# V once per 128 tokens, its rows moved to the key groups by transfers within SBUF

## The chip, the cores and the metric

The kernel runs on one core of a Trainium2 chip. The metric is the device time of one execution in microseconds (us): the median of repeated runs, and beside it one execution that the hardware profiler recorded, whose span and traces are quoted below.

## The reference

One transformer block with adaptive layer norm. The input `x` is 2048 tokens of 448 features; a conditioning vector `c` gives six modulation vectors through `silu(c) @ w_mod`. The first half is a sliding, dilated attention with 16 heads of 28 features, in which each token looks at itself and at seven earlier tokens, two apart; the second half is an MLP of width 1792.

```python
h = _layernorm(x) * (1 + ca) + sa
qkv = h @ wqkv                                  # 2048 x 3 x 16 x 28
idx = pos[:, None] - off[None, :]               # off = 0, 2, ..., 14
logits = einsum('bhsd,bhswd->bhsw', q, k[idx]) * 28 ** -0.5
o = einsum('bhsw,bhswd->bhsd', softmax(where(idx >= 0, logits, -1e9)), v[idx])
x = x + ga * (o @ wo)
h = _layernorm(x) * (1 + cb) + sb
y = _layernorm(h)
x = x + gb * (gelu(y @ w1 + b1) @ w2 + b2)
```

## The kernel before, in words

**Streams and tiles.** Since the offsets are all even, the even and the odd tokens are two independent streams (`NS` = 2) of 1024 tokens, in which a token looks at itself and the seven before it (`WIN` = 8). A tile `p` is 128 tokens of each stream; there are eight. For each tile the kernel loads `x`, normalizes it, transposes it (on PE for tiles 0 to 3, by `DMA_TRANSPOSE` on SP's queue for 4 to 7), applies the modulation into `hT` (features on the partitions), and computes Q and K. For tiles 2 to 7 (`natural_qk`, lines 615 to 636) Q and K come out with tokens on the partitions and are transposed by two `DMA_TRANSPOSE` on SP's queue into `qT` and `kT`.

**Batches.** Attention (`attention`, line 686) goes in nine batches of 114 queries per stream: two groups `j` of 57 queries (`WQ`), and each group has its 64 keys (`WK`), since the first query needs seven earlier tokens. The keys of group 0 sit on partitions 0 to 63, those of group 1 on 64 to 127. A batch computes the logits (`lt`, L742), their exponentials on ACT (L749), the mask on DVE (L755), the sums (`pd`, L764) and the product with V (`po`, L775); ACT turns the sums into reciprocals (L784, L786) and DVE multiplies (`omul`, L792) into `qT`, from where the output projection reads. 

**V before.** For the product, V must lie in the same two groups: `vb` is 128 partitions of 64 + 64 keys, by streams, heads and 32 features. The seven keys at the seam lie in both groups. For batches 1 to 8 the copy `windows` (L694) first puts the two windows of `hT` side by side into `hw`; V of the batch is then one product per stream against `Wv` (L552 for three full row blocks, L558 for the rest of 64 rows), and ACT or DVE evacuates it into `vb` (L725, L728). Batch 0 (`DIRECT`) takes the windows straight out of `hT` with products of 64 columns each (L710).

**Behind attention.** The modulation rows `ga`, `sb`, `g2`, `gb` are made on PE (L645), evacuated by ACT into `mod_rows` (L650), stored by SP into a DRAM buffer `mod_hbm` (L652) and read back by SP, broadcast over the partitions, as `mod_bc` (L654). DVE multiplies `wo_s`, the output weights, by `ga` (`wo_scale`, L657). The output projection of tile `p` (`pw`, L807) needs `wo_s` so scaled and the batches that cover the tile; then come the residual and two layer norms on DVE (L814 and on), a transpose on SP's queue (`yT`, L838), and in three phases the MLP (`p`, L552, L558 and L887; gelu on ACT, L868).

**What sets the order.** Every piece is a numbered task with its engine or a choice of engines. Two tables written out in the file decide everything: `ORDER` is the sequence in which the tasks are issued (and with a letter the engine of a task that has a choice), `SLOTS` the buffer that each takes. Each engine and each DMA queue works through its own tasks in that order. Entries such as `243+5@243` put small products of zeros (L390) in front of a task. SP issues the loads, the transposes and the stores in one queue; ACT's queue has only the loads of `c` in it.

Of the kernel before, what the change touches and what calls it, by code (L numbers as in the profile page):

```python
# [37 lines left out]
ROOM = {"P": 4, "et": 2, "den": 2, "zy": 5, "h2": 3, "yT": 3, "hm": 2, "vb": 3, "xp": 3, "hw": 2}  # L38
SPLIT = 2
DIRECT = range(0, 1)  # L40
# [12 lines left out]
64 66 79 67 88:A 111 21 65 68+2@68 109 69 70 22 23 85:P 26 112 110 80 89:P 113 81 82 90 27 95+16@95 114 86 91 116 92 102  # L53
103 115 83 104 87:A 96 84 97 117:A 118 93:A 98 120:A 119 94:P 41 36 28 121:A 122 100 30 105 107 106 135 137 138 136 99
139 123+1@123 133 108 147 242:P 145 140 148 101 146 149 142 134 29 141 150 31 151 152 204 124 126 125 127 191 192 202 32
189:R 194 33 143:A 203 205 34 190 153 154 144 206 207 156 155:A 158 128 157:A 129 35 195 214 131 212 40 130 8 163 208
209 210:D 132 211 291 292 37 164 165 193 196 215 160 246 247 213 249 159 250 216 248 197 251 175 281 161 198 166 217 219
218 220 252 38 176 199 289 200 254 168 282 290 293 162 167 279 280 294 243+5@243 244 169 201 283 177 319:P 284 172 323
324 295 221 326 171 245:D 320 286 39 178 285 255 327 321 170 222 225 253 223 325 224 226 173 287 296 393 328 329 322 297
256 288 330 331 356 332 227 231 179 230 232 174 228 298 180 257 333 49 302:A 258 261 51 259 334 335 360 363 394 364 238  # L60
357 395 262 260 263 338 300:A 361 264 358 336 266 265 299:A 301:A 396 339 337 239 240 267 308 340 307 365 268 271 269
341 343 270 342 359 303 229 309 233 272 344 273 46 586:P 304 44 43 588 397 345 362 400 305 401 587 235 367 274 276 398
275 589 241 346 366 368 234 47 236 348 347 349 277:D 350 471:P 369 472 45 399 402 403 315 351 353 352 316 354:D 370 405
54 188 473 278 355 53 404 406 407 371 185 474 408 372 373 375 317 431 183 432 374 376 450 508:A 430 377 436 435 378 187
449 42 409 410 451 412 434 181 437 411 433 452 438 441 444 380 442 443 413 414 379 381 382 385 386 383 50 440 439 306
384 453 415 184 416 52 318 446 186 445 447 310 48 182 417 387 388 418 419 237 422 456 466 420 475 478 464 448 470 479
476 457 423 421 424 467 425 427 515 516 512 390 389 391:D 426 513 465 392 428:D 509 477 480 429 481 312 468 517 510 311
514 518 511:D 519 483 482 313:D 484 520 521 545 547 546 550 485 522 523 524 486 549 551 558 559 527 548 487 563 561 568
571 488 454 489 528 469 560 490 491 562 314 553 552 557 554 555 623:P 570 565 625 492 624 626 564 556 460 493 525 590
494 495 496 497 500 526 529 501 530 531 498 499 566 567 585 455 572 569 630 532 533 534 502 593 594 595 535 537 591 458  # L70
631 538 592 536 459 461 462 503 627 596 598 539 540 628 579 632 505 580 599 629 633 635 597 541 634 542 543:D 504 506:D
581 600 636 637 601 582 638 602 603 583 639 544 640 507 661 641 662 642 643 644 604 605 606 607 608 610 660 665 645 646
647 648 649 652 664 609 611 612 666 663 653 615 613 614 668 667 669 672 670 463 671 673 674 677 678 676 680 679 682 616
573 617 618 681 683 619 620 690 688 696 650 651 654 686 655 656 657 574 658:D 621:A 694 622 684 675 689 685 691 692 687
575 576 659 718 577 701 719 720 721 700 697 704 695 702 703 706 698 705 699 707 708 584 578 709 713 722 726 725 724 711
710 693 712 717 715 729 716 714 737 727 730 738 739 728 733 734 723 731 740 732 735 741 742 736 743 744
# [87 lines left out]
def kernel(  # L164
# [32 lines left out]
    def fixed(room, tiles):  # L197
        return P.buf(room, lambda k: tiles[k])
# [32 lines left out]
    one1 = cst.tile([1, 128], BF16, name="one1")  # L231
# [4 lines left out]
    warm_w = cst.tile([128, 512], BF16, name="warm_w")  # L236
# [6 lines left out]
    vbufs = [cst.tile([128, NS, H, HP], BF16, name=f"vb{i}") for i in range(ROOM["vb"])]  # L243
    wm_st = sb("hm", [128, 2 * KT - 2, D], BF16, "wm_st")
# [55 lines left out]
    def consts():  # L300
        for vb in vbufs:
            nc.vector.memset(vb[:, :, :, DH:HP], 0.0)
        nc.vector.memset(ones_k[:], 1.0)
        nc.vector.memset(ones_k[0:WIN - 1, 1, :], 0.0)
# [90 lines left out]
    def c_cols():  # L395
        for k in range(KT):
            nc.tensor.matmul(psc.t[:, 0, 128 * k:128 * k + 128], lhsT=c_row[0:1, k * 128:(k + 1) * 128], rhs=one1[:], start=True, stop=True)
# [284 lines left out]

    def attention(i, tbl, prev_w1):
        q00 = i * SBQ
        ps_ = covers(q00 - (WIN - 1), q00 + SBQ + WK - WQ)
        kc = LEAD + q00 - (WIN - 1)
        vb = fixed("vb", vbufs)
        pv = psum("pv")
        if i not in DIRECT:
            hw = sb("hw", [128, KT, NS, 2, WK], BF16, "hw")  # L690

            def windows(copy):
                for j in range(2):
                    copy(out=hw.t[:].rearrange("p k s j c -> p (k s) j c")[:, :, j], in_=hT[:, :, kc + j * WQ:kc + j * WQ + WK])  # L694

            add("DVE", 0.46, lambda: windows(nc.vector.tensor_copy), port=True, reads=["pads"] + [f"h{kt}_{p}" for kt in range(KT) for p in ps_],
                bufs=[hw], fills=[hw], name="windows",
                alt={"ACT": (1.12, lambda: windows(nc.scalar.copy)), "POOL": (1.18, lambda: windows(nc.gpsimd.tensor_copy))})
            summed([(lambda s=s: pv.t[:, s, 0:D], lambda kt, rows, s=s: hw.t[rows, kt, s].rearrange("p j c -> p (j c)"),
                     lambda kt, rows: Wv[rows, kt, :]) for s in range(NS)], 0.1895, ["wv", "wvr0", "wvr1"],  # L700
                   [pv, vb, hw], [pv], f"v{i}")
        else:
            def vmm(kts, first):

                for s in range(NS):
                    for kt in kts:
                        rest = kt == KT - 1
                        rows = slice(KS * s, KS * s + KS) if rest else slice(0, 128)
                        for j in range(2):
                            nc.tensor.matmul(pv.t[WK * j:WK * j + WK, s, 0:D], lhsT=hT[rows, NS * kt + s, kc + j * WQ:kc + j * WQ + WK],  # L710
                                             rhs=Wv[rows, kt, :], start=first and kt == kts[0], stop=not first and kt == kts[-1],
                                             tile_position=(rows.start, WK * j))

            def v_last():
                vmm(range(KT - 1), True)
                vmm([KT - 1], False)

            def v_first():
                vmm([KT - 1], True)
                vmm(range(KT - 1), False)  # L720

            add("PE", 7 * 0.1895 + 0.1, None, reads=["pads", "wv", "wvr0", "wvr1"] + [f"h{kt}_{p}" for kt in range(KT) for p in ps_], bufs=[pv, vb],
                fills=[pv], instr=32, name=f"v{i}",
                alt={"PE": (7 * 0.1895 + 0.1, v_last, "128x64", "64x64"), "PE2": (7 * 0.1895 + 0.1, v_first, "64x64", "128x64")})
        add("ACT", 0.80, lambda: nc.scalar.copy(out=vb.t[:, :, :, 0:DH],  # L725
                                                in_=pv.t[:, :, 0:D].rearrange("p s (h d) -> p s h d", h=H)),
            reads=["vpad"], bufs=[pv, vb], fills=[vb], name="evac_v",
            alt={"DVE": (1.0, lambda: nc.vector.tensor_copy(out=vb.t[:, :, :, 0:DH],  # L728
# [237 lines left out]
```

## Time and profile before

| | us |
|---|---|
| median of 3 runs | 168.84 (168.84 to 168.95) |
| the profiled execution | 169.01 |
| its span in the trace | 167.3 |
| PE busy | 161.9 of the span |
| DVE, ACT, POOL busy | 121.0, 104.4, 48.4 |

The span runs from the first to the last instruction in the trace; 1.7 us of the profiled execution lie around it. Busy times of PE are of pipelined products, so a full PE is not yet a PE at its peak. The chain of work that ended last, and the timelines of PE, DVE, ACT and SP's queue, say more than the busy shares: they tell which wait stood at the end of each stage.

### The profile page before, as it was taken

Reading aid. Unit: us, or ns where it says so; the run is one execution under the profiler, and the core shown is the slowest. Engines: PE = TensorE matmul, PEld = TensorE weight load, DVE = VectorE, ACT = ScalarE, POOL = GpSimd, SP = SyncE. Lnnn points to the kernel's source line nnn. Section 1 sums busy time; section 2 is a strip of 40 time slices with the busy share of each in tenths; the row PEclk is TensorE's granted clock in tenths of the full one; section 3 lists DMA queues with packets and bytes.
Section 4 is the critical chain, followed back from the end, with each engine's and each line's share of the span. In section 5 each row is a group of like instructions: output and inputs, shape, how many; then the busy total and the mean of one; then the engine's idle time right before and its main releaser. Section 6 shows DMA issues by size and latency. Waiting matters only on the chain.

```text
span 167.3 us, 4993 instructions
## 1 busy us (share of the span) xinstructions
PE 161.9 (97%) x2121; PEld 84.5 (51%) x2121; DVE 121.0 (72%) x297; ACT 104.4 (62%) x145; POOL 48.4 (29%) x77
## 2 busy tenths in 40 slices
PE   6999999999999999999999999999999999999992
PEld 4767745455545443355544345464335554444651
DVE  6969999898999799978849679869797714020041
ACT  3267999777899976897872698670566100637300
POOL 5025514420157004180006574200304800090000
PEclk9999999999999999999999999999999999999999
DMA  5999839898997789206750000084000330023011
GB/s 156 299 276 319 323 73 135 187 214 203 158 276 205 157 184 239 52 0 35 151 67 2 4 0 4 0 76 109 4 0 0 65 63 0 4 106 113 0 69 41
DMA packets 33462, 18.26 MB, mean 109 GB/s; under 512 B 26395, under 2 KB 32480, under 8 KB 33440
## 3 DMA queue, kind: packets, MB, share of 16 engines
q1 hardware_dynamic: 33436, 17.95, 48.9%
q8 instruction: 16, 0.26, 0.7%
q14 instruction: 6, 0.05, 0.1%
q10 hardware_dynamic: 4, 0.00, 0.0%
HBM read 9.81 MB, written 1.84 MB: 70 GB/s over the span
## 4 chain that ended last, share of the span: by engine, by line
PE 87%; DMA 5%; SPq 2%; DVE 2%; ACT 2%; issue 0%; ACTq 0%
PE p L887 26%; PE p L552 22%; PE pq L552 10%; PE pw L807 7%; PE pv L552 5%; PE p L558 4%; PE lt L742 3%; DMA wqk_st<-in_A_wqkv_dram 3%; PE po L775 3%; PE pq L558 2%; DMA kT<-zy 2%; PE pd L764 1%; ACT et L749 1%; PE pv L710 1%; PE pv L558 1%; PE ptr L539 1%
## 5 line engine op out<-in xcount | busy, mean ns | idle before, releaser
L868 ACT ACTIVATE hm<-p,b_col 128x512 bf16<-128x512 f32 x56 | 34.0, 690 | 34.0 <-PE p L558 29.6
L887 PE MATMUL p<-w_s,hm 128*128 128x448 bf16 (+1 forms) x238 | 44.3, 342 | 0.0
L552 PE MATMUL p<-yT,w_s 128*128 128x512 bf16 x168 | 38.6, 380 | 0.0
L478 POOL TENSOR_TENSOR rs_all<-tv_all,neg_half 128x2 f32<-128x2 f32 x22 | 18.2, 830 | 56.7 <-DVE tv_all L476 56.5
L887 PEld LDWEIGHTS <-hm 128*128 128x128 bf16 x238 | 22.8, 98 | 19.1 <-issue 0.2
L893 DVE TENSOR_TENSOR x_all<-p,x1p 128x896 bf16<-128x896 f32 (+2 forms) x10 | 9.0, 904 | 25.2 <-PE p L887 25.2
L552 PEld LDWEIGHTS <-w_s 128*128 128x128 bf16 x168 | 15.8, 98 | 21.0 <-issue 3.4
L462 DVE BATCH_NORM_STATS2 stt<-x_all 128x6 f32<-128x448 bf16 x32 | 18.9, 616 | 0.3
L749 ACT ACTIVATE et<-lt 128x928 bf16<-128x928 f32 x18 | 16.3, 942 | 2.6 <-PE lt L742 2.5
L845 POOL TENSOR_TENSOR x1p<-x_all,gbb_bc 128x448 f32<-128x448 bf16 x16 | 16.4, 1049 | 0.0
L552 PE MATMUL pq<-wqk_st,hT 128*128 128x448 bf16 x72 | 15.5, 354 | 0.0
L807 PE MATMUL pw<-wo_s,qT 128*128 128x448 bf16 x64 | 12.9, 353 | 0.0
L814 DVE TENSOR_TENSOR x_all<-pw,x_all 128x896 bf16<-128x896 f32 x8 | 8.7, 1084 | 4.1 <-PE pw L807 4.1
L755 DVE TENSOR_TENSOR et<-et,mask 128x928 bf16<-128x928 bf16 x18 | 11.1, 634 | 0.7 <-ACT et L749 0.6
L792 DVE TENSOR_TENSOR qT<-po,den 128x912 bf16<-128x912 f32 x9 | 9.8, 1103 | 1.7 <-ACT den L786 1.2
L784 ACT ACTIVATE den<-pd 128x928 f32<-128x928 f32 x9 | 8.5, 944 | 4.1 <-PE pd L764 4.1
L823 DVE TENSOR_TENSOR h<-h,mod_bc 128x896 bf16<-128x896 bf16 x16 | 10.7, 668 | 0.4
L552 PE MATMUL pv<-Wv,hw 128*128 128x448 bf16 x48 | 10.4, 353 | 0.0
L632 ACT CAST zy<-pq 128x896 bf16<-128x896 f32 x11 | 9.9, 911 | 0.5 <-PE pq L552 0.2
L482 DVE TENSOR_SCALAR zy<-h,mvs,rs_all 128x448 bf16<-128x448 bf16 x16 | 7.9, 532 | 2.5 <-POOL rs_all L478 2.4
L786 ACT ACTIVATE den<-den,den_bias 128x928 f32<-128x928 f32 x9 | 9.6, 1068 | 0.2
L462 DVE BATCH_NORM_STATS2 stt<-h 128x6 f32<-128x448 bf16 x16 | 9.5, 617 | 0.2
(117 smaller groups left out, 190.2 us busy)
## 6 DMA issues: line engine op xcount, KB each, us to landing
w_s<-in_B_w_dram SPq DMA_DIRECT2D x7, 224.0 KB, 3.2
out_dram<-x_all SPq DMA_DIRECT2D x7, 224.0 KB, 2.1
x_all<-in_A_x_dram SPq DMA_DIRECT2D x3, 448.0 KB, 6.8
wmod<-in_w_mod_dram SPq DMA_DIRECT2D x3, 448.0 KB, 6.6
w_s<-in_B_w_dram SPq DMA_DIRECT2D x3, 448.0 KB, 4.6
wqk_st<-in_A_wqkv_dram SPq DMA_DIRECT2D x3, 225.0 KB
wm_st<-in_w_mod_dram SPq DMA_DIRECT2D x1, 672.0 KB
x_all<-in_A_x_dram SPq DMA_DIRECT2D x2, 224.0 KB, 3.8
```

Source lines behind the costliest of these rows:

```text
L462: add("DVE", 0.53, lambda: nc.vector.bn_stats(out=stt[:, w, b, :], in_=src()), reads=reads, bufs=bufs, after=early if w == b == 0 else (), ...
L478: add("POOL", 0.55 + 0.17 * n, lambda: nc.gpsimd.tensor_tensor(out=r, in0=tv, in1=neg_half[:, 0:n], op=ALU.pow), reads=[f"tv{w}_{b0}", "ne ...
L552: nc.tensor.matmul(out(), lhsT=lhs(kt, slice(0, 128)), rhs=rhs(kt, slice(0, 128)), start=first and kt == 0, stop=not first and kt == KT - 2)
L558: nc.tensor.matmul(out(), lhsT=lhs(KT - 1, rows), rhs=rhs(KT - 1, rows), start=first, stop=not first, tile_position=(rows.start, 0))
L632: add("ACT", 0.80, lambda to=to, src=src: nc.scalar.copy(out=to(), in_=src()), bufs=[pq, st], reads=["zpad"], writes=[(st, 0)], name="evac ...
L749: exps.append(add("ACT", 0.83, lambda half=half, lt=lt: nc.scalar.activation(out=et.t[:, 2 * half:2 * half + 2].rearrange("p r m c -> p r ...
L755: nc.vector.tensor_tensor(out=ev, in0=ev, in1=mask[:], op=ALU.mult)
L807: nc.tensor.matmul(pw.t[:, s, 0:D], lhsT=qT[:, KT * s + ft, LEAD + 128 * p:LEAD + 128 * p + 128], rhs=wo_s[:, ft, :], start=(ft == 0), sto ...
L823: add("DVE", 0.55, lambda vec=vec, op=op: nc.vector.tensor_tensor(out=h2.t[:], in0=h2.t[:], in1=vec.unsqueeze(1).to_broadcast([128, NS, D] ...
L845: add("POOL", 1.0, lambda n=n: nc.gpsimd.tensor_tensor(out=x1p.t[:, n, :], in0=xn(p, n), in1=gbb2_bc[:], op=ALU.add), reads=[f"x{p}", "gbb ...
L868: gelus.append(add("ACT", 0.585, lambda f=f, a=a, p1=p1s[g]: nc.scalar.activation(out=hm.t[:, f].rearrange("p n c -> p (n c)"), in_=p1.t[: ...
L887: nc.tensor.matmul(p2.t[:, n, 0:c1 - c0], lhsT=hm.t[:, f, n, q * 128:(q + 1) * 128], rhs=w2_s[:, f, c0:c1], start=(f == parts[0][0]), stop ...
```

## The change

V is computed once per tile of 128 tokens, straight from `hT`, with the products of L552 and L558 that batches 1 to 8 had; it is evacuated into a new buffer `vn` (three of them, tokens on the partitions in their natural order). For each batch, transfers within SBUF then copy rows of `vn` into the two groups of `vb`: each transfer takes a run of rows that lies within one tile and one group, 2 KB a row. That makes 26 runs of keys (of 1 to 64 rows) and one filler of two rows at the end of batch 8, where the window goes past the last token; in batch 0 DVE puts zeros into the first seven rows (`vzero`). Six of the transfers are issued by ACT, the others by SP. `windows`, `hw` and the direct products of batch 0 are gone. Two small buffers shrink (`one1` from 128 to 16 columns, `warm_w` from 512 to 256), the products of zeros become 48 where they were 46, and `ORDER` and `SLOTS` are new throughout, so that tasks of all engines stand in another order.

```diff
-ROOM = {"P": 4, "et": 2, "den": 2, "zy": 5, "h2": 3, "yT": 3, "hm": 2, "vb": 3, "xp": 3, "hw": 2}
+ROOM = {"P": 4, "et": 2, "den": 2, "zy": 5, "h2": 3, "yT": 3, "hm": 2, "vb": 3, "xp": 3, "vn": 3}
-17 18 19 0 1 11 2 4 5 9 15 14 20 55+14@55 24 13 6 12 73 71 72 3 16 56 57 58 74 59 25 75 60 61 63+8@63 76 7 62 10 77 78
+14 15 16 0 1 11 12 6 13 17 9 5 4 55+11@55 71 56 2 73 74 3 57 18 19 20 72 58 59 75 60 192 62 61 25 63+12@63 64 10 7 8 24
...
-    one1 = cst.tile([1, 128], BF16, name="one1")
+    one1 = cst.tile([1, 16], BF16, name="one1")
-    warm_w = cst.tile([128, 512], BF16, name="warm_w")
+    warm_w = cst.tile([128, 256], BF16, name="warm_w")
+    vns = [cst.tile([128, NS, H, HP], BF16, name=f"vn{i}") for i in range(ROOM["vn"])]
...
+    def v_tile(p):
+        vn = fixed("vn", vns)
+        pv, c0 = psum("pv"), LEAD + 128 * p
+        summed([(lambda s=s: pv.t[:, s, 0:D], lambda kt, rows, s=s: hT[rows, NS * kt + s, c0:c0 + 128],
+                 lambda kt, rows: Wv[rows, kt, :]) for s in range(NS)], 0.1895, ["wv", "wvr0", "wvr1"] + [f"h{kt}_{p}" for kt in range(KT)],
+               [pv], [pv], f"v{p}")
...
     def attention(i, tbl, prev_w1):
...
-        if i not in DIRECT:
-            hw = sb("hw", [128, KT, NS, 2, WK], BF16, "hw")
...
-            summed([(lambda s=s: pv.t[:, s, 0:D], lambda kt, rows, s=s: hw.t[rows, kt, s].rearrange("p j c -> p (j c)"),
...
+        def move(rows, p, r0):
+            vn = v_of[p]
+            vk.append((vb, len(vk)))
+            n = rows.stop - rows.start
+            go = lambda e: e.dma_start(out=vb.t[rows], in_=vn.t[r0:r0 + n])
+            add("SP", 0.5, lambda: go(nc.sync), bufs=[vb, vn], writes=vk[-1:], xfer=0.05 + 0.006 * n, name=f"vm{i}",
+                alt={"ACT": (0.42, lambda: go(nc.scalar))})
+
+        for j in range(2):
+            lo = q00 + WQ * j - (WIN - 1)
+            at = WK * j - lo
...
+            for p in covers(lo, lo + WK):
+                a, b = max(lo, 128 * p), min(lo + WK, 128 * p + 128)
+                move(slice(at + a, at + b), p, a - 128 * p)
+            if lo + WK > SL:
+                move(slice(at + SL, at + lo + WK), NP - 1, 0)
...
-        lt_mms.append(add("PE", 0.55, pmm, reads=[(et, 0), (et, 1)], bufs=[et, vb, po], fills=[po], mode="64x32", instr=128,
+        lt_mms.append(add("PE", 0.55, pmm, reads=[(et, 0), (et, 1)] + vk, bufs=[et, vb, po], fills=[po], mode="64x32", instr=128,
```

Two places show what the new order does around the first output projection. The first is SP's queue, from the store of the modulation rows on. Before:

```order
L652 DMA mod_hbm<-mod_rows 4x448
L531 DMA_TRANSPOSE zT<-zy_100 128x8x128
L374 DMA wo_s<-in_A_wo_dram 28x4x448
L654 DMA mod_bc<-mod_hbm 128x1792
L635 DMA_TRANSPOSE kT<-zy_97 128x8x128
```

After the change (`vb` and `vn` are buffers of three; the first number of a shape is the rows, each of 1024 bf16 numbers):

```order
L653 DMA mod_hbm<-mod_rows 4x448
L636 DMA_TRANSPOSE qT<-zy_99 128x8x128
L711 DMA vb_112<-vn_117 43x1024
L711 DMA vb_114<-vn_115 29x1024
L375 DMA wo_s<-in_A_wo_dram 28x4x448
L655 DMA mod_bc<-mod_hbm 128x1792
L711 DMA vb_114<-vn_117 35x1024
```

Between the store of the rows and their reading back there were a transpose and a load; now there are a transpose, two moves (43 rows for batch 1, 29 rows for batch 2) and a load. The second place is ACT, from the evacuation of a Q or K tile to the reciprocals of batch 0. Before:

```order
L632 CAST zy_101<-pq 128x32x28
L650 ACTIVATE mod_rows<-pb,one_cb 128x448
L784 ACTIVATE den<-pd 128x928
L786 ACTIVATE den<-den,den_bias 128x928
L784 ACTIVATE den<-pd 128x928
```

After the change:

```order
L633 CAST zy_100<-pq 128x32x28
L693 CAST vn_117<-pv 128x32x28
L693 CAST vn_116<-pv 128x32x28
L711 DMA vb_113<-vn_116 57x1024
L711 DMA vb_112<-vn_116 21x1024
L711 DMA vb_113<-vn_116 64x1024
L651 ACTIVATE mod_rows<-pb,one_cb 128x448
L781 ACTIVATE den<-pd 128x928
```

Two evacuations of V and three moves now stand ahead of `mod_rows`.

More of the change, by code (lines that the diff above doesn't have):

```diff
@@ L56 @@
[L56 to L60, printed above, removed]
@@ L300, in consts @@
     def consts():
[L301 to L302 removed]
+        for vn in vns:
+            nc.vector.memset(vn[:, :, :, DH:HP], 0.0)
         nc.vector.memset(ones_k[:], 1.0)
@@ L681 @@
     exps, lt_mms, w1_mms, gelus = [], [], [], []
+    v_of = {}
+    def v_tile(p):
[4 more added lines that the diff above has]
+               [pv], [pv], f"v{p}")
+        out, src = lambda: vn.t[:, :, :, 0:DH], lambda: pv.t[:, :, 0:D].rearrange("p s (h d) -> p s h d", h=H)
+        add("ACT", 0.80, lambda: nc.scalar.copy(out=out(), in_=src()), reads=["vpad"], bufs=[pv, vn], fills=[vn], name="evac_v",
+            alt={"DVE": (1.0, lambda: nc.vector.tensor_copy(out=out(), in_=src()))})
+        v_of[p] = vn
     def attention(i, tbl, prev_w1):
@@ L686, in attention @@
         kc = LEAD + q00 - (WIN - 1)
+        for p in ps_:
+            if p not in v_of:
+                v_tile(p)
         vb = fixed("vb", vbufs)
-        pv = psum("pv")
-        if i not in DIRECT:
-            hw = sb("hw", [128, KT, NS, 2, WK], BF16, "hw")
[L692 to L698, printed above, removed]
-            summed([(lambda s=s: pv.t[:, s, 0:D], lambda kt, rows, s=s: hw.t[rows, kt, s].rearrange("p j c -> p (j c)"),
[L700 to L728, printed above, removed]
-                                                            in_=pv.t[:, :, 0:D].rearrange("p s (h d) -> p s h d", h=H)))})
+        vk = []
+        def move(rows, p, r0):
[5 more added lines that the diff above has]
+                alt={"ACT": (0.42, lambda: go(nc.scalar))})
```

45 lines of the change are left out of this document (24 added, 21 removed), and 18 rows, old and new, of tables (ORDER, SLOTS).

## The prediction

> **What bounds the kernel now.** I read the page first, its busy times and its chain of work that ended last.
>
> ```profile
> span 167.3 us, 4993 instructions
> ...
> PE 161.9 (97%) x2121; PEld 84.5 (51%) x2121; DVE 121.0 (72%) x297; ACT 104.4 (62%) x145; POOL 48.4 (29%) x77
> ...
> PE 87%; DMA 5%; SPq 2%; DVE 2%; ACT 2%; issue 0%; ACTq 0%
> PE p L887 26%; PE p L552 22%; PE pq L552 10%; PE pw L807 7%; PE pv L552 5%; PE p L558 4%; PE lt L742 3%; DMA wqk_st<-in_A_wqkv_dram 3%; PE po L775 3%; PE pq L558 2%; DMA kT<-zy 2%; PE pd L764 1%; ACT et L749 1%; PE pv L710 1%; PE pv L558 1%; PE ptr L539 1%
> ```
>
> PE is the bound: 87% of the chain. What is taken from PE comes off the time one for one, as long as PE finds its operands ready; what makes PE wait is added one for one. So two questions decide: how much work leaves PE, and whether the moves, which now stand between V and `po`, reach PE or one of its feeders late.
>
> Next come the timelines, for the stage in which PE has least slack. The first lines are of PE, then of DVE, then of SP's queue (start, duration).
>
> ```profile
> 34.03 0.71 PE L775 MATMUL po<-et,vb 64*32 64x57 bf16 x64
> 36.12 0.75 PE L775 MATMUL po<-et,vb 64*32 64x57 bf16 x64
> 38.44 3.19 PE L807 MATMUL pw<-wo_s,qT 128*128 128x448 bf16 x16
> ```
> ```profile
> 36.84 0.49 DVE L694 COPY hw<-hT 128x512 bf16<-128x512 bf16 x2
> 37.25 1.15 DVE L657 TENSOR_TENSOR wo_s<-wo_s,mod_bc 128x896 bf16<-128x896 bf16 x2
> 38.48 1.11 DVE L792 TENSOR_TENSOR qT<-po,den 128x912 bf16<-128x912 f32 x1
> ```
> ```profile
> 27.59 1.24 SPq L635 DMA_TRANSPOSE kT<-zy  x1
> 28.92 0.57 SPq L652 DMA_DIRECT2D mod_hbm<-mod_rows  x1
> 29.59 1.25 SPq L531 DMA_TRANSPOSE zT<-zy  x1
> 30.90 0.56 SPq L374 DMA_DIRECT2D wo_s<-in_A_wo_dram  x1
> 31.55 0.36 SPq L654 DMA_DIRECT2D mod_bc<-mod_hbm  x1
> ```
>
> The reader is to see that the scaling of `wo_s` ends at 37.25 + 1.15 = 38.40 and the first output projection starts at 38.44: PE takes it the moment DVE has it. So `mod_bc`, from its issue at 31.55 through the scaling, is already at PE's elbow. DVE came to the scaling straight from the windows (36.84 + 0.49), so `mod_bc` landed within 37.25 - 31.55 = 5.7 us of its issue, how much earlier the trace doesn't show.
>
> **What leaves PE.** The rows of V's products:
>
> ```profile
> L552 PE MATMUL pv<-Wv,hw 128*128 128x448 bf16 x48 | 10.4, 353 | 0.0
> L558 PE MATMUL pv<-Wv,hw 64*128 64x448 bf16 x16 | 2.7, 353 | 0.0
> ```
> ```profile
> 16.43 1.57 PE pv L710 x16
> ```
>
> Eight batches had 48 + 16 products; eight tiles will have the same 48 + 16 of the same shape. The direct batch goes: 1.57 us on the chain (the last row). The two products of zeros more stand at the start, where PE waits for loads anyway; I cost them at nothing, and at 0.2 us if that cover is gone (0.11 each, below). Rounded: **-1.5**.
>
> ```profile
> 14.10 0.11 PE pq L390
> ```
>
> **What leaves the other engines.** The windows and one evacuation of nine:
>
> ```profile
> L694 POOL COPY hw<-hT 128x512 bf16<-128x512 bf16 x10 | 5.9, 621 | 1.7 <-ACT hT L508 1.2 <-PE pv L552 0.5
> L725 ACT CAST vb<-pv 128x896 bf16<-128x896 f32 x7 | 6.4, 908 | 0.0
> L694 ACT COPY hw<-hT 128x512 bf16<-128x512 bf16 x2 | 1.1, 628 | 0.0
> L694 DVE COPY hw<-hT 128x512 bf16<-128x512 bf16 x4 | 1.0, 284 | 0.0
> ```
>
> 5.9 us of POOL, 1.1 of ACT, 1.0 of DVE and 0.9 of ACT. None of it ends a wait of PE in the chain, so it brings nothing by itself. In return DVE gets one short fill of zeros and, by the new order, evacuates one Q or K tile more (1.1 us); I count that as even.
>
> **What the moves cost their issuers.** ACT issues six. Its issues in this trace:
>
> ```profile
> 0.80 0.51 ACTq L351 DMA_DIRECT2D c_row<-in_c_dram  x1
> 25.96 0.64 ACT L650 ACTIVATE mod_rows<-pb,one_cb 128x448 bf16<-128x448 f32 x1
> ```
>
> Three stand ahead of `mod_rows`: 3 x 0.51 = 1.5 us, with two evacuations of 0.9. `mod_rows` ended at 26.6 and its store went out only at 28.92, so 2.3 us of this are hidden by SP's earlier rows; I keep 28.92 for the store and let the rest go into the range. SP issues 21 moves at about 0.57 us, some 12 us of issue, in a queue whose next rows mostly wait for data.
>
> **What the moves cost in the queue.** No transfer within SBUF but the transposes is in the trace, so the duration must be bounded. A row is 2 KB. The 16 DMA engines at their best:
>
> ```profile
> DMA  5999839898997789206750000084000330023011
> GB/s 156 299 276 319 323 73 135 187 214 203 158 276 205 157 184 239 52 0 35 151 67 2 4 0 4 0 76 109 4 0 0 65 63 0 4 106 113 0 69 41
> ...
> q10 hardware_dynamic: 4, 0.00, 0.0%
> ```
>
> The fifth slice moved 323 GB/s at a share of 8 tenths (80 to 90%): 323 / 16 / 0.85 = 24 GB/s for one engine, 0.086 us for a row of 2 KB. The two moves that SP issues ahead of `mod_bc` have 43 and 29 rows. Spread over 16 engines they take 72 x 0.086 / 16 = 0.4 us; on one engine 3.7 + 2.5 = 6.2 us. I take **one engine**: whole rows can be shared equally only among a number of engines that divides them, and 43 and 29 are prime. Every large transfer of this trace has 128, 64 or 28 rows; the nearest row to one that can't be shared is that of the queue q10, ACT's: it held two transfers of one row each, and 4 packets, two per transfer, so such a transfer didn't touch 16 engines. That is thin, and the other end stays a rival.
>
> [...]
>
> Now the queue, by the new order and the durations above: store 28.92 to 29.5, transpose of Q 1.24 to 30.8, the move of 43 rows from 30.8, of 29 rows from 31.4, the load of `wo_s`, `mod_bc` at about 32.6. Transposes of Q land 3.1 us after their issue:
>
> ```profile
> qT<-zy SPq DMA_TRANSPOSE x6, 3.1
> mod_bc<-mod_hbm SPq DMA_DIRECT2D x1, 448.0 KB
> ```
>
> so the engine comes to the 43 rows between 31.3 (issued) and 32.6 (the transpose has landed), say 31.9. It is through with both at 38.1. I take it that each engine works off SP's queue in order; then its share of `wo_s` (98 KB) and `mod_bc` (448 KB) comes behind the rows: 546 KB / (16 x 24) = 1.4, to 39.5. The scaling takes 1.15, to 40.7. PE would be at the output projection at about 38.4, as before: of what it does ahead of that, the direct V (1.57) gives way to a plain product (1.33), and the new order exchanges a Q or K tile. Wait: 40.7 - 38.4 = **+2.3**. Its ends are nothing (the moves are spread) and, with 20 GB/s per engine, the mean of the row below (327 / 16), 7.2 us for the 72 rows, +3.3.
>
> ```profile
> 10.00:20.00 10.00, 9.62 (x159) 6.71 (x160) 8.62 (x30) 7.72 (x13) 4.26 (x8) 1.00 1.06 327
> ```
>
> Behind the waiting scaling on DVE stand `omul` of batch 2 and the residual of tile 0, which need the same projection, so this delay is not paid twice. The waits of `po` 1 and `po` 2 for those rows lie ahead of it on PE and are contained in it. Later moves have slack: the second and third phase come behind tens of microseconds of MLP, and SP's queue is nearly idle there.
>
> **The sum.** 169.0 (profiled) - 1.5 + 2.3 = 169.8; the median of the runs lies 0.2 below the profiled execution: **169.6**.
>
> **The rivals.**
>
> A. *The moves are spread and land in time* (0.30). For it: 0.4 us of transfer, and PE's work is 1.5 us shorter. Against it: the prime counts. The later place of `mod_bc` (32.6 for 31.55) can cost up to 1.0 if it used all its 5.7 us. 169.0 - 1.5 = 167.5 to 168.5, as a median 167.4 at the likeliest; faster.
>
> [...]
>
> B. *One engine, but only `po` waits* (0.14): the big loads get round the busy engine. The 43 rows are there at 35.6, the 29 at 38.1; `po` 1 and 2, at 34.03 and 36.12 before, come some 0.7 later by the new order, so the second waits 38.1 - 36.9 = 1.2 in all. 169.0 - 1.5 + 1.2 - 0.2 = 168.5: no difference that shows. It decides if the scaling starts at 38 or earlier.
>
> C. *The first engines become the bound up to the MLP* (0.10). The moves of 58, 34 and 62 rows go in two shares of 29, 17 and 31 rows, 2.5, 1.5 and 2.7 us each, on the same first engines that carry the MLP's weights, with the share of the DMA engines at 9 tenths between 42 and 50 us. If the weights or `yT` then come 1.5 late at the first MLP product as well: 171.1. It decides from the point where the last `w_s` load lands after PE's arrival, near 60 us.
>
> **How the numbers follow.** Forecast 0.46, A 0.30, B 0.14, C 0.10. The forecast's own range is 168.8 to 170.7 (wait of 1.5 to 3.3). A measurement of this kernel can tell some 0.2% (0.34 us) from no change. Faster: A, 0.30. Same: B, 0.14. Slower: the forecast and C, 0.56. The range must reach into A and C: 167.2 to 171.2.
>
> **What would show it.** Right: the scaling of `wo_s` waits for a DMA and starts near 39.5, with a gap on PE of about 2 us ahead of the first `pw`; V's products take 13.1 us with no L710 kind; PE's busy time falls by 1.5. Rival A: no gap, the first `pw` at or before 38.5. B: gaps ahead of `po` alone. C: a gap at the first MLP product near 60. The forecast is wrong if short moves land within 3 us whatever their row count, or if PE comes to the projection later for another reason (the three issues on ACT, say), so that nothing waits for `mod_bc`.

## The result, and the profile after

The changed kernel takes 179.17 us (median of four runs, 178.73 to 179.49) against 168.89: a ratio of 1.060 (interval 1.057 to 1.063), 10.3 us slower. The sign was forecast, the size by far not: the prediction said 169.6, and its range ended at 171.2. Executions that took over 1.5% longer than the fastest of the same kernel are left out of the times and ratios here and below.

The page of the changed kernel, with the lines that answer to those of before:

```profile
span 177.6 us, 4993 instructions
...
PE 165.4 (93%) x2107; PEld 85.4 (48%) x2107; DVE 121.8 (69%) x291; ACT 102.8 (58%) x141; POOL 43.1 (24%) x71
...
PE 79%; DMA 11%; issue 3%; DVE 3%; ACT 2%; SPq 1%; ACTq 0%
```

PE has 14 products fewer and is busy 3.5 us longer; in the chain, PE's share fell from 87 to 79% and that of DMA rose from 5 to 11%. So PE both waits more and works more slowly. Where it waits, in the timeline of PE (start, duration, and in brackets the idle time ahead and what ended it):

```profile
16.63 0.70 PE L739 MATMUL lt<-qT,kT 28*64 28x58 bf16 x64
...
31.17 0.64 PE L772 MATMUL po<-et,vb 64*32 64x57 bf16 x60 [0.60 <-DMA vb<-vn]
...
35.08 0.83 PE L739 MATMUL lt<-qT,kT 28*64 28x58 bf16 x64 [1.24 <-DMA qT<-zy]
...
38.31 0.68 PE L772 MATMUL po<-et,vb 64*32 64x57 bf16 x64 [0.86 <-ACT zy L633]
...
39.22 0.38 PE L761 MATMUL pd<-et,ones_k 64*32 64x464 bf16 x6
42.84 0.57 PE L761 MATMUL pd<-et,ones_k 64*32 64x464 bf16 x2 [3.24 <-issue]
...
46.36 4.18 PE L804 MATMUL pw<-wo_s,qT 128*128 128x448 bf16 x16
...
65.77 0.75 PE L772 MATMUL po<-et,vb 64*32 64x57 bf16 x64 [1.19 <-DMA vb<-vn]
...
71.92 0.61 PE L559 MATMUL p<-yT,w_r 64*128 64x512 bf16 x4 [0.74 <-DMA yT<-zy]
```

The stretch from the first `lt` to the first MLP product was 60.59 - 15.99 = 44.6 us and is now 71.92 - 16.63 = 55.3; what follows takes 105.7 (106.7 before). Before the change, its two ends and the whole of it (in the last row the length, then the busy time of PE; the granted clock is third from the right):

```profile
15.99 0.44 PE L742 MATMUL lt<-qT,kT 28*64 28x58 bf16 x32
60.59 2.75 PE L552 MATMUL p<-yT,w_s 128*128 128x512 bf16 x12
```
```profile
15.99:60.59 44.60, 44.30 (x918) 23.75 (x918) 41.34 (x104) 40.40 (x50) 14.01 (x20) 1.00 0.91 194
```

After the change, the whole stretch and one piece of it:

```profile
16.63:71.92 55.29, 47.38 (x905) 24.00 (x905) 43.22 (x99) 36.42 (x44) 7.77 (x14) 0.94 0.89 163
```
```profile
40.00:50.00 10.00, 7.16 (x86) 3.13 (x87) 3.52 (x5) 5.04 (x6) 0.00 (x0) 0.66 0.96 157
```

The six waits add up to 7.9 us, where 0.3 were idle before. PE is busy 47.4 us against 44.3. So 10.7 us = 7.6 more idle + 3.1 more busy. Most of the 3.1 is the clock: between 40 and 50 us it was 0.66 of full on average, and in windows of a quarter microsecond it is 0.50 from 41.6 to 48.4 us. It fell 2 us into the longest wait. PE worked 5.5 us at half the clock, an estimated 2.8 us longer than at full clock; `pw` took 4.18 us for 3.19.

The two feeders that the prediction spoke of, ACT's queue, then the first rows of SP's, then DVE's scaling:

```profile
26.35 2.26 ACTq L711 DMA_DIRECT2D vb<-vn  x3
28.65 0.64 ACT L651 ACTIVATE mod_rows<-pb,one_cb 128x448 bf16<-128x448 f32 x1 [2.33 <-DMA vb<-vn]
```
```profile
29.31 0.58 SPq L653 DMA_DIRECT2D mod_hbm<-mod_rows  x1
29.99 1.28 SPq L636 DMA_TRANSPOSE qT<-zy  x1
31.31 1.35 SPq L711 DMA_DIRECT2D vb<-vn  x2
32.72 0.54 SPq L375 DMA_DIRECT2D wo_s<-in_A_wo_dram  x1
33.36 1.03 SPq L655 DMA_DIRECT2D mod_bc<-mod_hbm  x1
```
```profile
42.55 1.16 DVE L658 TENSOR_TENSOR wo_s<-wo_s,mod_bc 128x896 bf16<-128x896 bf16 x2 [2.22 <-DMA mod_bc<-mod_hbm]
```

The scaling waited for `mod_bc`, as forecast, until 9.2 us after its issue (at most 5.7 before). But the scaling ended at 43.7, and `pw` began only at 46.36, right behind `po` of batch 2 and with no wait of its own: PE was held by other things.

The trace also holds every DMA packet with its time and size, which no view lists one by one, and these packets show the engine that the prediction took. The 72 rows of the moves of 43 and 29 rows ran one behind the other from 33.75 to 40.21 us. Of the 128 rows of `mod_bc` (3584 bytes each), 120 were over by 37.92, and the last eight ran one by one from 40.52 to 41.62, behind the moves. In the kernel before, all 128 ran from 32.55 to 34.95: `mod_bc` was there 2.3 us ahead of the scaling.

### The profile page after: what moved, and what is told of

The parts are those of the page before. It is cut to its first block, busy times and chain, and to the rows that moved or that the text cites. A ratio compares the mean times of both kernels' runs of the same rounds, so it can differ in the third digit from the quotient of the medians.

```text
span 177.6 us, 4993 instructions
## 1 busy us (share of the span) xinstructions
PE 165.4 (93%) x2107; PEld 85.4 (48%) x2107; DVE 121.8 (69%) x291; ACT 102.8 (58%) x141; POOL 43.1 (24%) x71
## 3 DMA queue, kind: packets, MB, share of 16 engines
q1 hardware_dynamic: 34514, 19.71, 55.3%
## 4 chain that ended last, share of the span: by engine, by line
PE 79%; DMA 11%; issue 3%; DVE 3%; ACT 2%; SPq 1%; ACTq 0%
PE p L884 21%; PE p L553 21%; PE pq L553 7%; PE pw L804 6%; DMA vb<-vn 5%; PE pv L553 5%; PE p L559 4%; DMA yT<-zy 4%; DMA qT<-zy 3%; PE lt L739 2%; PE po L772 2%; PE ps_col L391 2%; PE ps_c L391 1%; PE pq L559 1%; PE ptr L540 1%
## 5 line engine op out<-in xcount | busy, mean ns | idle before, releaser
L479 POOL TENSOR_TENSOR rs_all<-tv_all,neg_half 128x2 f32<-128x2 f32 x22 | 16.9, 766 | 83.5 <-DVE tv_all L477 83.4
L890 DVE TENSOR_TENSOR x_all<-p,x1p 128x896 bf16<-128x896 f32 (+2 forms) x10 | 9.0, 902 | 25.5 <-PE p L884 25.4
L842 POOL TENSOR_TENSOR x1p<-x_all,gbb_bc 128x448 f32<-128x448 bf16 x16 | 17.0, 1082 | 0.1
L553 PE MATMUL pq<-wqk_st,hT 128*128 128x448 bf16 x72 | 16.8, 372 | 0.0
L553 PEld LDWEIGHTS <-hT 128*128 128x128 bf16 x120 | 10.9, 100 | 11.9 <-issue 3.7
L752 DVE TENSOR_TENSOR et<-et,mask 128x928 bf16<-128x928 bf16 x18 | 11.6, 669 | 5.9 <-ACT et L746 5.9
L633 ACT CAST zy<-pq 128x896 bf16<-128x896 f32 x10 | 9.1, 910 | 9.3 <-DMA yT<-zy 4.6
L804 PE MATMUL pw<-wo_s,qT 128*128 128x448 bf16 x64 | 14.1, 371 | 0.0
L820 DVE TENSOR_TENSOR h<-h,mod_bc 128x896 bf16<-128x896 bf16 x16 | 11.6, 727 | 0.3
L553 PE MATMUL pv<-Wv,hT 128*128 128x448 bf16 x48 | 10.4, 354 | 0.0
```

What stands on the lines that cost most here:

```text
L479: add("POOL", 0.55 + 0.17 * n, lambda: nc.gpsimd.tensor_tensor(out=r, in0=tv, in1=neg_half[:, 0:n], op=ALU.pow), reads=[f"tv{w}_{b0}", "ne ...
L553: nc.tensor.matmul(out(), lhsT=lhs(kt, slice(0, 128)), rhs=rhs(kt, slice(0, 128)), start=first and kt == 0, stop=not first and kt == KT - 2)
L752: nc.vector.tensor_tensor(out=ev, in0=ev, in1=mask[:], op=ALU.mult)
L804: nc.tensor.matmul(pw.t[:, s, 0:D], lhsT=qT[:, KT * s + ft, LEAD + 128 * p:LEAD + 128 * p + 128], rhs=wo_s[:, ft, :], start=(ft == 0), sto ...
L820: add("DVE", 0.55, lambda vec=vec, op=op: nc.vector.tensor_tensor(out=h2.t[:], in0=h2.t[:], in1=vec.unsqueeze(1).to_broadcast([128, NS, D] ...
L842: add("POOL", 1.0, lambda n=n: nc.gpsimd.tensor_tensor(out=x1p.t[:, n, :], in0=xn(p, n), in1=gbb2_bc[:], op=ALU.add), reads=[f"x{p}", "gbb ...
```

## The experiments

Three theories stood against each other. **1**: moves with badly shared row counts occupy one or two DMA engines, and everything else in the queue waits behind them. **2**: the DMA engines are full in that stretch, and 2.3 MB more cost time in whatever shape. **3**: each further issue costs its queue about 0.57 us, and what stands behind it comes later.

The start differs between the profiled runs by up to 3.3 us (first `lt` at 15.69 to 18.96; the load of `wm_st` lands at 6 to 7.5 us, for a reason that I haven't found, and in the latest of them the clock was halved for 3.4 us behind that wait as well), so beside the ratio stand the stretch from the first `lt` to the first MLP product in the profiled run, and what follows it.

| kernel | us | ratio to before | stretch | behind it |
|---|---|---|---|---|
| before | 168.89 | 1 | 44.6 | 106.7 |
| changed | 179.17 | 1.060 (1.057 to 1.063) | 55.3 | 105.7 |
| all uneven moves split | 175.22 | 1.039 (1.035 to 1.043) | 51.2 | 105.9 |
| 43 and 29 rows split | 172.40 | 1.022 (1.019 to 1.024) | 48.4 | 105.8 |
| no moves, zeros at the start | 168.71 | 1.001 (0.999 to 1.003) | 43.7 | 106.3 |
| no moves, zeros later | 168.90 | 1.002 (0.999 to 1.004) | 44.5 | 105.9 |
| split, Q's transpose first | 175.80 | 1.042 (1.035 to 1.048) | 51.6 | 105.7 |
| split, ACT's six on GpSimd | 172.24 | 1.020 (1.014 to 1.027) | 49.3 | 106.7 |
| mod_bc first | 178.41 | 1.057 (1.051 to 1.064) | 51.5 | 105.8 |
| all moves on GpSimd | 177.71 | 1.053 (1.045 to 1.061) | 49.1 | 111.7 |
| batches 0 to 4 on GpSimd | 172.80 | 1.024 (1.022 to 1.027) | 46.8 | 107.0 |
| 28 products more | 181.15 | 1.071 (1.065 to 1.078) | 56.7 | 106.2 |
| before + 18 of 64 bytes | 172.55 | 1.020 (1.012 to 1.027) | 46.8 | 106.6 |
| before + 18 even | 175.19 | 1.040 (1.034 to 1.046) | 51.5 | 107.6 |
| before + 18 uneven | 180.13 | 1.064 (1.054 to 1.073) | 54.9 | 106.5 |

### What one move costs by itself

```
     P.emit(filler)
+    nc.sync.dma_start(out=vbufs[1][0:64], in_=vbufs[0][0:64])
+    nc.sync.dma_start(out=vbufs[0][0:43], in_=vbufs[1][0:43])
...
```

> The kernel before with a chain of 13 moves behind its end, each reading what the one ahead wrote, of 64, 43, 48, 29, 32, 58, 62, 35, 57, 63, 16, 15 and 2 rows of 2 KB, so that the time from issue to issue is the duration of one move with nothing beside it. Theory 1: about 2 us and 0.086 us a row for each engine's share: 43 rows 5.7, 29 rows 4.5, 58 and 62 rows 4.5, 64, 48, 32, 16 and 15 rows 2.1 to 2.4, 35 and 63 rows 2.4 to 2.6. Against theory 1: the time follows the bytes, with 43 rows between 32 and 48. The whole is about 40 us longer than the kernel before.

SP's queue behind the end of the old kernel's work, where nothing else runs; each row waits until the one ahead has landed, and the rows are in the order 64, 43, 48, 29, 32, 58, 62, 35:

```profile
164.71 0.54 SPq L937 DMA_DIRECT2D vb<-vb  x1
167.06 0.68 SPq L938 DMA_DIRECT2D vb<-vb  x1
173.42 0.56 SPq L939 DMA_DIRECT2D vb<-vb  x1
175.69 0.59 SPq L940 DMA_DIRECT2D vb<-vb  x1
180.46 0.54 SPq L941 DMA_DIRECT2D vb<-vb  x1
182.40 0.63 SPq L942 DMA_DIRECT2D vb<-vb  x1
187.23 0.59 SPq L943 DMA_DIRECT2D vb<-vb  x1
192.23 0.78 SPq L944 DMA_DIRECT2D vb<-vb  x1
```

From start to start: 64 rows 2.35 us, 43 rows 6.36, 48 rows 2.27, 29 rows 4.77, 32 rows 1.94, 58 rows 4.83, 62 rows 5.00. 43 rows took longer than 64, so the bytes alone don't decide. Between 43 and 29 rows lie 1.59 / 14 = 0.114 us a row, over a base of 1.46; by that estimate two shares of 31 give 4.99, and 62 rows took 5.00, as 58 rows (two shares of 29) took 4.83 where 29 took 4.77. Beside the rows of 2 KB the trace has 1 packet of 4 bytes for 43 and for 29 rows, 16 for 48 and 32, 2 for 58 and 62, 7 for 35. I read their number as that of the engines, since the times fit it; in these seven moves it is the largest divisor of the row count up to 16. Theory 1 holds for one move alone, at a third more per row than I had taken (0.086); in the changed kernel the 72 rows took 6.46 us, 0.090 each.

### Splitting the uneven moves

```
-            go = lambda e: e.dma_start(out=vb.t[rows], in_=vn.t[r0:r0 + n])
+            def go(e):
+                for a, b in pieces(n):      # 43: 0-32, 32-43; 29: 0-16, 16-29
+                    e.dma_start(out=vb.t[rows.start + a:rows.start + b], in_=vn.t[r0 + a:r0 + b])
```

> The changed kernel with only the moves of 43 and 29 rows (batches 1 and 2) issued as two, 32 + 11 and 16 + 13. Theory 1: the first output projection, 7.9 us late, comes back to within 2 us of the kernel before (38.4 to 40.5), and what the MLP's start loses beside it, some 3.4 us, stays: 171 to 174. Theory 2 and 3: 178 to 180.

> The changed kernel with each move whose row count shares badly (43, 29, 58, 34, 62, 57, 35, 49, 63, 44 rows) issued as two: a multiple of 16 rows and the rest. Same rows and bytes, ten more issues. Theory 1 (43 and 29 rows go through one DMA engine, 58, 34 and 62 through two, and everything else in the queue waits behind them): most of the 10.3 us comes back, 169 to 172, with mod_bc landing within 6 us of its issue. Theory 2 (the DMA engines are full in that stretch, whatever the shape of the moves, since 2.3 MB more pass through them): 177 to 180. Theory 3 (each further issue costs its engine, about 0.57 us apiece): 180 or more.

Two moves of 27, issued as four, give 6.8 us of the 10.3 back (172.40, where theory 1 had 171 to 174). In PE's timeline of that kernel the hold ahead of the last products of `pd` has shrunk to 0.29, and `pw` is at full speed. The wait for `qT` is still there (1.56 for 1.24), so it isn't due to those two moves:

```profile
34.58 0.70 PE L748 MATMUL lt<-qT,kT 28*64 28x58 bf16 x64 [1.56 <-DMA qT<-zy]
...
38.38 0.37 PE L770 MATMUL pd<-et,ones_k 64*32 64x464 bf16 x2 [0.29 <-issue]
...
40.53 3.20 PE L813 MATMUL pw<-wo_s,qT 128*128 128x448 bf16 x16
```

Splitting the eight other uneven moves too makes it slower again, by 2.8 us: 175.22 lies in none of the three forecasts, but the direction is that of theory 3. SP issues almost without a pause there; the transpose of the MLP's input goes out at 60.55 us for 58.98, ACT then waits 2.9 us for it to leave its buffer, and PE stands 2.2 us behind ACT ahead of the second half of `pw`:

```profile
59.77 1.69 PE L813 MATMUL pw<-wo_s,qT 128*128 128x448 bf16 x8
61.29 1.30 PE L558 MATMUL pq<-wqk_st,hT 128*128 128x448 bf16 x6
64.75 2.48 PE L813 MATMUL pw<-wo_s,qT 128*128 128x448 bf16 x8 [2.16 <-ACT zy L638]
```

### What V per tile brings without its moves

```
-            go = lambda e: e.dma_start(out=vb.t[rows], in_=vn.t[r0:r0 + n])
+            go = lambda e: None             # vb set to zeros: the attention's output is left out
```

> The changed kernel without its moves: the key groups are zeros, set once on GpSimd, so the attention's output is left out, while V is still computed per tile and evacuated. All theories: what V per tile brings alone, 1.5 us off PE, 167 to 168. If it stays above 170, the loss isn't the moves' but the new order's.

> As the run without moves, but the key groups are set to zeros by GpSimd where the first moves of batches 0 to 2 stood, not at the start, where the run without moves lost 1.3 us ahead of the first lt. The attention's output is again left out. If V per tile with the new order is worth what its products say: 167.0 to 167.6. If the new order itself costs something: 168.3 or more, with a gap on PE behind the first lt that the kernel before doesn't have.

In all there is no gain (168.71, where 167 to 168 was expected). The profiled runs of both started late (first `lt` at 17.58 and 18.33); from there to the end they took 150.0 and 150.4 us, the kernel before 151.3. These 0.9 to 1.3 us aren't all V's: the new order does six products of Q and K (0.8 us) ahead of the first `lt` that lay behind it before. So no run shows the 1.5 us as a gain of the whole; on the other side, the new order without the moves costs nothing. Why the load of `wm_st` lands late in these two stays open; five other kernels show it as well.

### Three rungs in the old kernel

```
+    # old kernel, V as it was; at the changed kernel's places
+    e.dma_start(out=scr[0:1, 32 * a:32 * a + 32], in_=ident[0:1, 0:32])                  # 64 bytes
+    e.dma_start(out=w2_s[a:a + n, c:c + 2, :], in_=Wv[128 - n:128, 0:2, :])              # n rows
```

> The kernel before, V as it was, with 18 transfers of 64 bytes that nobody reads: six on ACT and twelve on SP, where the changed kernel issues the moves of the first phase. Only issues and queue places, no bytes and no waits for data. Theory 3 (issue time on SP and ACT): some 0.57 us each, of which those in front of the transposes of Q, K and the MLP's input count: 171 to 174. Theories 1 and 2: 168.5 to 169.5.

> As the run with 18 transfers in the old kernel that nobody reads, with the row counts that share well in place of those that don't: 64, 16, 64, 64, 64, 16 on ACT; 48, 32, 32, 48, 64, 64, 16, 64, 16, 32, 16, 64 on SP (33 rows more in all, the same places). Theory 1 (few engines per transfer): from first lt to first MLP product it falls from 54.9 us to 47 to 49, close to the 46.8 of the 18 transfers of 64 bytes, about 172 to 174 in all. Theory 2 (bytes on full engines): it stays at 53 to 56, 178 to 181.

> As the run with 18 transfers of 64 bytes, but each has the row count of the changed kernel's move at that place (57, 21, 64, 64, 64, 15 on ACT; 43, 29, 35, 49, 64, 63, 6, 58, 1, 34, 20, 64 on SP) with rows of 1792 bytes; nobody reads them. Theory 1 (one-engine transfers hold what stands behind them): 174 to 178, with mod_bc late and the scaling of wo_s waiting, though no po waits for a move. If the loss comes only from po's own waits for its rows: 169 to 171.

The first MLP product in the three profiles, in this order (first `lt` at 15.69, 16.25 and 16.98), the first with its longest wait:

```profile
28.04 0.37 PE L566 MATMUL pq<-wqr_st,hT 64*128 64x448 bf16 x2 [1.67 <-ACT mod_rows L658]
...
62.44 2.75 PE L560 MATMUL p<-yT,w_s 128*128 128x512 bf16 x12
```
```profile
67.76 2.75 PE L559 MATMUL p<-yT,w_s 128*128 128x512 bf16 x12 [0.33 <-PE pw L814]
```
```profile
71.89 2.75 PE L559 MATMUL p<-yT,w_s 128*128 128x512 bf16 x12
```

Eighteen transfers that nobody reads cost the old kernel 11.2 us (10.3 in the stretch), as much as the change lost, and more than the 174 to 178 that theory 1 alone had for them. Neither V nor a wait of `po` for its rows is needed for a loss of this size. By the stretch the issues make 2.2 of it, the bytes in even rows 4.7, the uneven rows 3.4; by the medians, each against runs of the old kernel beside it, 3.6, 2.8 and 4.8. The sizes are loose (the profile with 64 bytes is of a run 1.9 us below its median, that with even rows of one 2.1 above, and each order reacts in its own way), but the intervals of the three ratios don't overlap: all three theories hold a part, and none holds alone.

### Is mod_bc what PE waits for?

```
-... 251:A 250 204 289 229 300 302 329 227 290 37 330:A 202 260 228 168 226 205 169 171 178 292
+... 251:A 37 178 250 204 289 229 300 302 329 227 290 330:A 202 260 228 168 226 205 169 171 292
```

> The changed kernel, moves whole, with the load of wo_s and mod_bc issued ahead of the moves of 43 and 29 rows on SP. The prediction's step taken literally (the scaling of wo_s is what PE waits for): the scaling starts near 37.5, not 42.6, and most of the 7.9 us at the first output projection comes back, 171 to 174. Rival (the one-engine moves hold PE by po of batches 1 and 2 as well, and by whatever else passes through that DMA engine): the scaling is early, PE isn't, 176 to 179.

The rows of `mod_bc` are over at 38.20 now, and the scaling no longer waits for a DMA. But it starts no earlier: DVE has `omul` of batch 1 to do first, which waits for `po`, and `po` for its own rows. DVE and PE of that kernel:

```profile
43.30 1.11 DVE L789 TENSOR_TENSOR qT<-po,den 128x912 bf16<-128x912 f32 x1 [2.90 <-PE po L772]
44.33 1.15 DVE L658 TENSOR_TENSOR wo_s<-wo_s,mod_bc 128x896 bf16<-128x896 bf16 x2
```
```profile
42.52 0.71 PE L772 MATMUL po<-et,vb 64*32 64x57 bf16 x64 [2.83 <-DMA vb<-vn]
...
47.04 3.20 PE L804 MATMUL pw<-wo_s,qT 128*128 128x448 bf16 x16
```

The time is the rival's: 178.41 against 179.17, with ratios whose intervals overlap. This profiled run started 2.3 us later than that of the changed kernel, so the places are to be counted from the first `lt` (18.96). Then the scaling starts after 25.4 us (25.9 in the changed kernel) and `pw` after 28.1 (29.7; 22.4 before the change): of the 7.3 us by which `pw` had slipped, 1.7 come back. The stretch is 3.8 us shorter (51.5), with no hold ahead of `pd` and the clock halved for 3.4 us in place of 6.8. How much of that the other runs share can't be told, since only one was profiled.

### The heads of two queues

In the kernel with 43 and 29 rows split:

```
-... 176 177 166 203 ...
+... 176 166 177 203 ...            # SP: the transpose of Q ahead of the store of mod_rows
```

> The kernel with 43 and 29 rows split, and on SP the transpose of Q issued ahead of the store of mod_rows, which waits for ACT's three issues. Theory 3 (issues at the head of a queue hold what stands behind them: the 1.6 us that lt2 waits for qT are the three issues on ACT): the transpose goes out near 27.6, not 29.7, lt2 waits no more, 170.6 to 171.2. Theory 2 (the transpose is slow because the DMA engines are full): no change, 172.2 to 172.6.

It became 3.4 us slower, which neither forecast had. `lt2` waits no more, but now `po` of batch 0 does, for moves that ACT had issued between 26.88 and 29.15; the DMA share from 30 to 34 us was 1.25 and 1.03:

```profile
34.93 0.64 PE L781 MATMUL po<-et,vb 64*32 64x57 bf16 x60 [3.78 <-DMA vb<-vn]
```

```
-                alt={"ACT": (0.42, lambda: go(nc.scalar))})
+                alt={"ACT": (0.42, lambda: go(nc.gpsimd))})
```

> The kernel with 43 and 29 rows split, and the six moves that ACT issued now issued by GpSimd; nothing else is moved. Theory 3 (ACT's three issues ahead of mod_rows hold the store and with it the transpose of Q): mod_rows starts as soon as its products end, the store and the transpose of Q go out about 1.3 us earlier, lt2 waits less, 170.5 to 171.3. Theory 2 (the transposes and the moves share full DMA engines, so what goes out earlier lands no earlier, or pushes the moves of batch 0 behind it as when the transpose of Q was put first): 172 to 175.

At its place theory 3 is right: `mod_rows` starts behind its products and not behind ACT's issues, and `lt2` no longer waits. In all nothing is gained: the two quickest runs, 171.77 and 172.70, stand level with the two splits (172.40), and the four spread from 171.8 to 176.2. In the profiled one, at 174.65, `po` of batches 2 and 4 now wait for moves:

```profile
27.78 0.63 ACT L656 ACTIVATE mod_rows<-pb,one_cb 128x448 bf16<-128x448 f32 x1 [1.30 <-PE pd L770]
```
```profile
39.53 0.67 PE L781 MATMUL po<-et,vb 64*32 64x57 bf16 x64 [1.27 <-DMA vb<-vn]
...
59.59 0.90 PE L781 MATMUL po<-et,vb 64*32 64x57 bf16 x64 [1.97 <-DMA vb<-vn]
```

### Another issuer

```
+            q = nc.gpsimd if i < 5 else nc.sync      # or nc.gpsimd for all nine batches
-            add("SP", 0.5, lambda: go(nc.sync), ...
+            add("SP", 0.5, lambda: go(q), ...
```

> The changed kernel, its 27 moves whole, all issued by GpSimd, which is idle three quarters of the time; SP and ACT issue what they did before the change. Theory 1 and 3 together (one-engine moves and issue time on SP and ACT are the loss, and a transfer from GpSimd is shared over the engines in some other way): 167.5 to 170. Theory 1 alone with the same sharing from GpSimd: mod_bc is still late behind 43 and 29 rows, 174 to 178. Theory 2 (full DMA engines): 177 to 180.

> The changed kernel, moves whole, those of batches 0 to 4 issued by GpSimd and those of batches 5 to 8 by SP and ACT as in the changed kernel. The all-GpSimd run had 49.1 us from first lt to first MLP product against 55.3 and lost some 5.9 us later, where its po waited for moves of the later batches. Theory 1 and 3: the first stretch stays at 49, the later loss goes, 172 to 173.5; still above the kernel before, since 18 moves among the transposes stay. If the later loss stays: 177 or more.

All moves on GpSimd end in theory 2's range, but not for its reason: the stretch falls to 49.1 us, and 5 us are lost behind it, where `po` of later batches waits for moves (2.86 and 1.04) and the clock halves again.

Issued by GpSimd, whole moves don't follow the times of SP's above: median times from issue to landing, all moves on GpSimd (128 KB are 64 rows, 86 KB 43, 58 KB 29):

```profile
vb<-vn POOLq DMA_DIRECT2D x8, 128.0 KB, 3.7
...
vb<-vn POOLq DMA_DIRECT2D x1, 86.0 KB, 3.7
...
vb<-vn POOLq DMA_DIRECT2D x1, 58.0 KB, 3.5
```

The other moves lie between 2.0 us (30 rows) and 7.0 us (58 rows).

With batches 0 to 4 there, `mod_bc` is issued at 31.07 (31.55 before the change), the scaling starts at 36.88, and the stretch falls to 46.8. What is left is 2.4 us of waits, the longest for a move again:

```profile
53.66 0.67 PE L773 MATMUL po<-et,vb 64*32 64x57 bf16 x64 [1.32 <-DMA vb<-vn]
```

At 172.80 it is no better than the two splits (172.40). No version here beats the kernel before.

### What holds eight products for 3.2 us

```
-... 333 335 336 ... 337 339 ...
+... 333 335 336 ... 337+28@337 339 ...      # 28 products of warm_w ahead of pd of batch 2
```

> The changed kernel with 28 useless products of 0.11 us ahead of pd of batch 2, into the same buffer, which pd overwrites: they fill the 3.2 us in which PE stands idle there. If that idle time is what halves the granted clock from 43 us on, the clock stays whole, the first output projection takes 3.2 us and not 4.2, and the kernel is 2 to 3 us faster, 176 to 177. If the clock drops for another reason, or PE can't run the products there, 179 to 182.

It came out slower, as the second branch has it: PE couldn't run the products there, and how it couldn't is the find. PE's timeline:

```profile
38.41 0.68 PE L772 MATMUL po<-et,vb 64*32 64x57 bf16 x64 [1.50 <-DMA vb<-vn]
...
39.32 1.22 PE L391 MATMUL pd<-warm_w 128*128 128x256 bf16 x6
42.87 4.30 PE L391 MATMUL pd<-warm_w 128*128 128x256 bf16 x22 [2.33 <-issue]
47.10 0.39 PE L761 MATMUL pd<-et,ones_k 64*32 64x464 bf16 x8
```

In the changed kernel six products of `pd` ran and the next were held; here six of the 28, which wait for nothing, and the next were held, until the same 42.9. So the hold belongs to a place in PE's instruction stream (instruction 1213 in its order, weight loads counted), not to what stands there. It is at the same place, after six products of `pd`, with the splits (0.29) and with both GpSimd kernels (1.89 and 0.68). The kernel without moves and with late zeros has one of 0.41 at instruction 1979. The clock fell to 0.50 at 39.6 us here, ahead of the hold and with PE at work: so the hold isn't what halves it, or not alone; waits of 1.09 and 1.50 us lie ahead of it. The page's queue of instructions moved 0.26 MB in 16 packets, 16 KB each:

```profile
q8 instruction: 16, 0.26, 0.6%
```

That PE stood waiting for one of these packets isn't shown; their times fit it in part only. With the splits one ran until 36.80, and the hold ended 1.6 us later; with all moves on GpSimd and with batches 0 to 4 there it ended 1.3 and 1.5 us behind such a packet. In the changed kernel the packet was over at 37.88, but the hold lasted until 42.84; here with 28 products more they are 38.02 and 42.87. So what kept PE for those 3 us and more wasn't the packet's own transport. The engine with the moves of 43 and 29 rows ran its last row of 2 KB until 42.02 and 42.33, just ahead of the end of the hold. But with `mod_bc` first PE passed the place at 43.65 without a hold, while rows of the moves ran until 44.81. That splitting the two moves ends the long hold is shown; by which way they hold PE stays open.

## Why the prediction was wrong

- **"-1.5 leaves PE."** The products are as told: V's after the change are 48 + 16 (10.4 and 2.5 us), without the direct ones. No run shows the gain: the kernels without moves are at 168.71 and 168.90, and the 0.9 to 1.3 us behind their first `lt` hold 0.8 of shifted order.
- **One engine for 43 and 29 rows.** Right, and nearly in size: their rows ran from 33.75 to 40.21, where the forecast had 31.9 to 38.1.
- **"`mod_bc` ... is already at PE's elbow."** A misreading, though it did little harm: in the kernel before, `mod_bc` was there 2.3 us ahead of the scaling, and PE was busy with products of Q and K until `pw`. So the start of `pw` at the end of the scaling shows no wait for it.
- **"Wait = +2.3", PE waits for the scaling.** This is the step that failed. The scaling waited as told (42.55, forecast 39.5), but PE reached `pw` only at 46.36, where the forecast had 38.4, and found `wo_s` ready: it had lost more ahead of it. In place of one wait of 2.3 us the runs showed 7.6 us more of waiting, in six places, and 3.1 us more of busy time, some 2.8 of it by the clock. Splitting the two moves alone gave 6.8 us back; the hold of 3.24 and the slow clock, some 6.0 of the 10.7 us, went with it. Issuing `mod_bc` ahead of them gave back 0.8 in the median and 3.8 in the stretch of the profiled run. I had let the slow engine delay one consumer. It also delays the readers of the moves themselves (2.83 at `po` of batch 1 in the run with `mod_bc` first), and with those moves whole PE was held at `pd`, in a way that stays open.
- **"The waits of `po` 1 and `po` 2 ... are contained in it."** They weren't: what PE loses ahead of `pw` moves `pw` itself, and the stretch with it.
- **"2.3 us of this are hidden; I keep 28.92."** Nearly right for the store, which went out 0.4 late, but not for what stands behind it. ACT's three issues took 2.26 us, and `mod_rows`, behind them, moved from 25.96 to 28.65. The transpose of Q, behind the store, went out at 29.99 and landed 5.0 us after its issue (3.1 before): 1.24 us at `lt2`.
- **"Later moves have slack."** True for phases 2 and 3 (105.7 us behind the first MLP product, 106.7 before), not for batch 4: 1.19 at `po`, and 0.74 for `yT` at the first MLP product. The place is rival C's, which had 0.10 and a price of 1.5; that the moves of 58, 34 and 62 rows are the cause isn't shown.
- **Cost of issues.** I called SP's queue nearly free. Eighteen transfers of 64 bytes, twelve on SP and six on ACT, cost 2.2 to 3.6 us in the old kernel; 1.67 of it is a wait for `mod_rows`, behind ACT's issues, so the run gives no price for SP's alone.

The range failed for the same reason: every rival priced one wait at one place.

## What to carry to other kernels

The transfers added to this crowded stretch cost what they displaced in the DMA engines and in their issuing queues, not only what their own readers waited: put dummy transfers of the same shape into the old kernel and see, before the work is moved (here 10.3 us in the stretch, for the 10.7 of the change). Of the seven row counts timed above, issued by SP, 32, 48 and 64 took 1.94 to 2.35 us, and 29, 43, 58 and 62 took 4.77 to 6.36; that speaks for multiples of 16, but each split is one issue more, so split first those that go through one engine: here that gave 6.8 us, and splitting the rest cost 2.8. And the price of PE's waits is not only their length: here a hold of 3.24 us came with 6.8 us at half the clock, an estimated 2.8 us more of work.

## What the runs showed of the hardware

- PE's granted clock fell to 0.50 for 3.3 to 3.4 us, or for 6.8, in stages where PE stood idle: in the changed kernel from 41.6 to 48.4 us, with all moves on GpSimd from 39.7 to 43.1 us, behind a hold of 1.89 (`pw` took 4.32 us for 3.20). Behind gaps of 1.56 (the two splits) and 1.67 (18 transfers of 64 bytes) it stayed whole. The length of one gap doesn't decide it: with 18 even transfers the clock fell at 39.7 us, and no gap in the 30 us ahead of it was longer than 1.22.
- PE was held at one place in its instruction stream (instruction 1213) without a wait that the profile shows, listed as idle ended by "issue": 3.24 us in the changed kernel, 2.33 with 28 products more, 1.89 and 0.68 in the two GpSimd kernels, 0.29 with the two splits.
- Issued by SP, 43 rows of 2 KB took 6.36 us and 48 rows 2.27, with nothing beside them; issued by GpSimd in the full kernel, 43 and 64 rows landed alike, 3.7 us after their issue.
